# q and k of batches 2 to 7 made feature-major by TensorE transposes instead of a DMA crossbar round trip

## Chip, core and metric

One core of one Trainium2 chip runs the kernel in a single launch. The metric is the device time of that core in microseconds. The times of a kernel are given as the median of its runs; the profile is one execution, recorded by the hardware profiler.

Engines: PE is TensorE's matmuls, PEld its weight loads, DVE is VectorE, ACT ScalarE, POOL GpSimd, SP SyncE, which here only issues transfers. Each engine takes its instructions in order. PSUM is the memory that TensorE writes; SBUF is the on-chip memory for the rest.

## What is computed

Blockwise causal attention over 8 batches of 8 heads, 576 positions and 64 features, followed by a gated linear unit whose gate is a causal convolution of five taps:

```
scores = scale * np.matmul(q, k.transpose(0, 1, 3, 2))     # scale = 1/8
mask = block_i >= block_j                                  # blocks of 64 positions
attn = softmax of scores where mask
x = np.matmul(attn, v)                                     # (8, 8, 576, 64)
x = x.transpose(0, 2, 1, 3).reshape(8, 576, 512)
gate_pre[:, s] = sum over k of conv_w[k] * x[:, s + k - 4]
gate = 1 / (1 + exp(-gate_pre))
out = (gate * (x @ w_val)) @ w_out                         # float32, (8, 576, 512)
```

## The kernel before

Two heads are worked on at a time, 64 features each, so that a pair fills the 128 partitions. A step t is one pair of heads: batch b = t // 4, pair n = t % 4; there are 32 steps with scores, and nine more (LAG = 9), as the gated unit runs nine steps behind. The gated unit's step m = t - 9 makes one group of 128 features of one batch.

**What a step holds**, in the order in which it is written and in which TensorE takes it:

- `scores(t, 0)`: score matmuls k x q into the PSUM tile `ps` (pool psS, two buffers), and the exponentials on ACT into `pt` (L205)
- on every second step, `load_pair` loads q and k of a half-batch `hb` (two pairs of heads) on SP, and GpSimd casts them to half precision into `q16` (L118); `load_v` and `cast_v` do the same for v once a batch
- `project`: four matmuls into `ot`, a copy by ACT into `ob` (L393), and a transfer of `ob` to the output, issued from ACT's own queue (L394)
- on the first step of a batch, `den`: 88 small matmuls into `dn`, the sums of the softmax of the batch before, and their reciprocal `ri` on DVE; `spread` copies it to `rqs` on GpSimd a step later
- on the last step of a batch and on the first of the next, `pv` for two pairs: a shuffle of the reciprocals into `rb` on DVE, matmuls into `x`, and a product of `x` and `rb` into `xb` on DVE
- `scores(t, 1)` and `scores(t, 2)`: the other score matmuls and exponentials (L231, L205)
- from t = 9 on, `gate`: ten matmuls into `cv` and a tanh on ACT; then `val`: eight matmuls into `vp` and a product on DVE into `gv`

The tiles `tr`, `dn`, `x`, `cv`, `vp` and `ot` share one PSUM pool, psG, of four buffers; a tile gets a buffer when the reader of an earlier one is done with it.

**Order.** Every matmul and transpose on TensorE goes through `tc.keep_in_program_order`. So does every DVE operation that is written as `vec.…` (class `Ordered`; its operations carry line 56), and every load on SP (`load`, line 46). Engines wait for each other by semaphores that the framework puts in.

**Feature-major q and k.** The scores need q and k with features on partitions: `qkT`, a tile of two buffers, one per batch. There are two ways to it. Half-batches 0 to 3 (batches 0 and 1) take `trans(hb, part)`: six TensorE transposes of 128 x 128 into the PSUM tile `tr` (L169), and one or two copies from there into `qkT`, on DVE but for one on ACT. Three parts make a half-batch. Half-batches 4 to 15 (batches 2 to 7) take the other way: `store_rows(hb)` writes the cast q and k to a tensor `qk_scratch` in device memory by two transfers on SP, on even steps, and `cross(hb)` issues two crossbar transposes on SP on the following odd step (L157), which read the scratch and write `qkT`. Half-batch hb serves the steps 2 hb and 2 hb + 1; it is stored in step 2 hb - 4 and crossed in step 2 hb - 3. The number XB = 2 sets where one way ends and the other begins.

The list `tr` of a step holds its parts: on an even step parts 1 and 2 of half-batch t/2 + 1, on an odd step part 0 of half-batch (t + 3)/2. Until t = 8 they are put between the parts of the scores; from t = 9 on, where a step has any, one would follow `gate`, and the next `val`.

Of the kernel before, what the change touches and what calls it, by code (L numbers as in the profile page):

```python
# [10 lines left out]
def kernel(  # L11
# [20 lines left out]
    nc = tc.nc  # L32
    fp32 = mybir.dt.float32
    fp16 = mybir.dt.float16
# [4 lines left out]
    B, H, S, D = q.shape  # L39
    NT = B * 4  # L40

    def mm(**kw):
        tc.keep_in_program_order(nc.tensor.matmul(**kw))  # L43

    def load(**kw):
        tc.keep_in_program_order(nc.sync.dma_start(**kw))  # L46
# [36 lines left out]
    qkp = ctx.enter_context(tc.tile_pool(name="qkp", bufs=2))  # L83
# [21 lines left out]
    q16 = {}  # L105
# [15 lines left out]
    def load_v(b):  # L121
        st = vstp.tile([128, 36, 64], fp32, tag="vst")
        load(out=st[:, :, :], in_=v[b].rearrange("h s d -> (h s) d").rearrange(
            "(t p) d -> p t d", p=128))
        vsts[b] = st
# [14 lines left out]


    qkT = {}
    scr = nc.dram_tensor("qk_scratch", [B, 2, 4, S, 128], fp16, kind="Internal")

    def store_rows(hb):
        b, half = divmod(hb, 2)
        for w in range(2):
            load(out=scr[b, w, 2 * half:2 * half + 2].rearrange("n (x c) d -> x n (c d)", c=9),
                 in_=q16[hb, w][:, :, :, :].rearrange("p c z d -> p (c z d)"))

    def cross(hb):

        b, half = divmod(hb, 2)
        if b not in qkT:
            qkT[b] = qkp.tile([128, 2, 4, S], fp16, tag="qkT", name="qkT")
        for w in range(2):
            tc.keep_in_program_order(nc.sync.dma_start_transpose(  # L157
                out=qkT[b][:, w, 2 * half:2 * half + 2, :].rearrange("p n s -> p (n s)"),
                in_=scr[b, w, 2 * half:2 * half + 2].rearrange("n s d -> (n s) d")))

    def trans(hb, part):

        b, half = divmod(hb, 2)
        if b not in qkT:
            qkT[b] = qkp.tile([128, 2, 4, S], fp16, tag="qkT", name="qkT")
        tr = psG.tile([128, 6, 128], fp16, tag="G")
        slots = [divmod(6 * part + s, 9) for s in range(6)]
        for s, (w, c) in enumerate(slots):
            tc.keep_in_program_order(nc.tensor.transpose(  # L169
                out=tr[:, s, :], in_=q16[hb, w][:, c, :, :], identity=ident16[:, :]))  # L170
        for w in range(2):
            ss = [s for s in range(6) if slots[s][0] == w]
            if ss:
                c0 = slots[ss[0]][1]
                evac = nc.scalar.copy if hb == 0 and part == 1 else vec.tensor_copy
                evac(
                    out=qkT[b][:, w, 2 * half:2 * half + 2, :].rearrange(
                        "p n (x c) -> p n x c", c=9)[:, :, :, c0:c0 + len(ss)],
                    in_=tr[:, ss[0]:ss[-1] + 1, :].rearrange("p c (x n) -> p n x c", n=2))

# [6 lines left out]
    def first_q(h, i):  # L187
        return 2 * i + 1 + h

    def scores(t, part):  # L190
        b, n = divmod(t, 4)
        if part == 0:
            pts[t] = ptp.tile([128, 2880], fp16, tag="pt", name="pt")
        pt = pts[t]
        hs = (slice(0, 64), slice(64, 128))
        qT = [qkT[b][hs[h], 0, n, :] for h in range(2)]
        kT = [qkT[b][hs[h], 1, n, :] for h in range(2)]

        def full(ps, h, i, lo):
            f = 64 * first_q(h, i)  # L200
            mm(out=ps[:, h, lo:lo + S - f], lhsT=kT[h][:, f - 64:f + 64], rhs=qT[h][:, f:S],
               start=True, stop=True, skip_group_check=True)

        def ex(o, src, w):
            nc.scalar.activation(out=pt[:, o:o + w], in_=src, func=AF.Exp, bias=0.0,  # L205
                                 scale=0.125)

        if part == 0:
            ps = psS.tile([128, 2, 512], fp32, tag="S")
            full(ps, 0, 0, 0)  # L210
            full(ps, 1, 0, 0)
            full(ps, 1, 3, 448)
            ex(0, ps[:, :, :], 1024)
            ps = psS.tile([128, 2, 512], fp32, tag="S")
            full(ps, 0, 1, 0)
            full(ps, 1, 1, 0)
            full(ps, 0, 3, 384)
            full(ps, 1, 2, 320)
            ex(1024, ps[:, :, :], 1024)
            return  # L220
        q4 = [x.rearrange("d (j x) -> d j x", x=64) for x in qT]
        if part == 1:
            ps = psS.tile([128, 2, 512], fp32, tag="S")
            full(ps, 0, 2, 0)
            mm(out=ps[64:128, 1, 0:256], lhsT=kT[1][:, 0:64], rhs=q4[1][:, 1:8:2, :],
               start=True, stop=True, skip_group_check=True)
            for i in range(4):
                f = 64 * (2 * i + 1)
                mm(out=ps[0:64, 1, 64 * i:64 * i + 64], lhsT=kT[1][:, f:f + 64],
                   rhs=qT[1][:, f:f + 64], start=True, stop=True, skip_group_check=True)  # L230
            nc.scalar.activation(  # L231
                out=pt[:, 2048:2560].rearrange("p (h x) -> p h x", h=2),
                in_=ps[:, :, 0:256], func=AF.Exp, bias=0.0, scale=0.125)
            return
        ps = psS.tile([128, 2, 512], fp32, tag="S")
        mm(out=ps[64:128, 0, 0:320], lhsT=kT[1][:, 0:64], rhs=q4[1][:, 0:9:2, :],
           start=True, stop=True, skip_group_check=True)
        for i in range(5):
            f = 128 * i
            mm(out=ps[0:64, 0, 64 * i:64 * i + 64], lhsT=kT[0][:, f:f + 64],  # L240
               rhs=qT[0][:, f:f + 64], start=True, stop=True, skip_group_check=True)
        ex(XO, ps[:, 0, 0:320], 320)
# [178 lines left out]
    def load_pair(hb):  # L421
        if hb < 2 * B:
            for w in range(2):
                load_qk(hb, w)
# [3 lines left out]
    for part in range(3):  # L428
        trans(0, part)
# [2 lines left out]

    proj = []
    LAG = 9
    XB = 2
    for t in range(NT + LAG):
        b, r = divmod(t, 4)
        m = t - LAG
        hb = (t + 3) // 2 if t % 2 else t // 2 + 1
        tr = [(hb, part) for part in ((1, 2), (0,))[t % 2]] if hb < 2 * XB else []  # L440
        if t == 0:
            tr.insert(0, (1, 0))
        if t < NT:
            scores(t, 0)
        if t % 2 == 0:
            load_pair(t // 2 + 3)
        if t % 2 == 0 and 2 * XB <= t // 2 + 2 < 2 * B:
            store_rows(t // 2 + 2)
        if t % 2 == 1 and 2 * XB <= t // 2 + 2 < 2 * B:
            cross(t // 2 + 2)  # L450
        if r == 0 and b < B:
            load_v(b)
        if t in (2, 3, 6, 7):
            weights(t // 4, t % 2 * 2)
        if r == (2 if b else 1) and b < B:
            cast_v(b)
        if t <= 4:
            conv_weights(t - 1)
        if proj:
            project(*proj.pop(0))  # L460
        if r == 0 and 1 <= b <= B:
            den(b - 1)
        if m < 0 and tr:
            trans(*tr.pop(0))
        for n in range(2):
            if r == 3 and 1 <= b <= B:
                pv(4 * b - 4 + n)
            if r == 0 and 2 <= b <= B + 1:
                pv(4 * b - 6 + n)
            if n == 0 and t < NT:  # L470
                if 0 <= m:
                    scores(t, 1)
                    scores(t, 2)
                else:
                    scores(t, 1)
                    if tr:
                        trans(*tr.pop(0))
        if m < 0 and t < NT:
            scores(t, 2)
        if r == 1 and 1 <= b <= B:  # L480
            spread(b - 1)
        if 0 <= m < NT:
            gate(*divmod(m, 4))
        if tr:
            trans(*tr.pop(0))
        if 0 <= m < NT:
            val(*divmod(m, 4))
            u, i = divmod(m, 8)
            if i == 3:
                proj.extend((u, j) for j in range(4))  # L490
            if i == 7:
                proj.extend((u, j) for j in range(4, 9))
        if tr:
            trans(*tr.pop(0))
        if proj:
            project(*proj.pop(0))
# [32 lines left out]
```

## Time and profile before

| | |
|---|---|
| median of 3 runs | 280.26 us (279.19 to 280.95) |
| the profiled run | 280.95 us, its span 278.8 us |
| mean granted TensorE clock | 0.920 |
| PE busy | 217.4 us, 78% |
| PEld busy | 146.6 us, 53% |
| ACT busy | 139.3 us, 50% |
| DVE busy | 118.2 us, 42% |
| POOL busy | 116.6 us, 42% |
| transfers from SP's queue (q1) | 44.57 MB, 61.4% of 16 engines |
| transfers from ACT's queue (q10) | 9.45 MB, 9.1% |
| scratch stores | 24 of 288 KB, 5.6 us from issue to landing |
| crossbar transposes | 24, 4.4 us from issue to landing |

Busy time is time with an instruction in work; matmuls are pipelined, so their durations overlap, and the time that a run of them takes is read from the start of one to the start of the next. In the rows of a timeline the first number is the start in microseconds from the start of the span, the second the duration; `[9.24 <-ACT pt L205]` says that the engine was idle for 9.24 us before this row, until ACT's instruction on `pt` released it. In the rows of groups, `x8 | 7.6, 950` is eight instructions, 7.6 us in all, 950 ns each.

The page's 40 slices (7 us each) show how the clock and the transfers run along the span:

```profile
PEclk9999975599989799995699777999999999999999
DMA  6998589999868995999899989988730210031214
```

The transfer engines are nearly full for the first two thirds, as long as q and k are loaded, and the granted clock dips in that part several times.

### The profile page before, as it was taken

How to read it: one execution, taken by the hardware profiler on the slowest of the kernel's cores; microseconds unless marked ns; L12 is line 12 of the kernel's file. 1: busy time of each engine (PE TensorE's matmuls, PEld its weight loads, DVE VectorE, ACT ScalarE, POOL GpSimd, SP SyncE). 2: the span in 40 equal slices, each digit the busy share in tenths (PEclk: the TensorE clock that was granted, in tenths of full speed). 3: DMA queues.
4: the chain of work that ended last, by engine and by line, in shares of the span. 5: the costliest groups of instructions: out<-in, count | busy, mean ns of one | idle time of the engine just before them, and what ended most of it. 6: DMA issues, size and time to landing. Idle time of an engine off the chain costs nothing.

```text
span 278.8 us, 6862 instructions
## 1 busy us (share of the span) xinstructions
PE 217.4 (78%) x2848; PEld 146.6 (53%) x2848; DVE 118.2 (42%) x249; ACT 139.3 (50%) x233; POOL 116.6 (42%) x168
## 2 busy tenths in 40 slices
PE   0599873968486889880798485989998998899994
PEld 0465642846273457540476243665467457567671
DVE  2278972445152145610248010672257136648230
ACT  2558681377143585450563534546664682342433
POOL 5455953864474357073807363139005800400000
PEclk9999975599989799995699777999999999999999
DMA  6998589999868995999899989988730210031214
GB/s 188 347 269 245 171 283 195 312 245 299 179 212 157 355 282 214 243 296 137 319 246 281 186 282 274 278 181 160 156 128 2 78 75 5 24 126 41 100 54 188
DMA packets 56745, 54.46 MB, mean 195 GB/s; under 512 B 30597, under 2 KB 39813, under 8 KB 56714
## 3 DMA queue, kind: packets, MB, share of 16 engines
q1 hardware_dynamic: 51520, 44.57, 61.4%
q10 hardware_dynamic: 5194, 9.45, 9.1%
q8 instruction: 22, 0.36, 0.5%
q14 instruction: 9, 0.07, 0.1%
HBM read 30.42 MB, written 16.52 MB: 168 GB/s over the span
## 4 chain that ended last, share of the span: by engine, by line
PE 55%; ACT 14%; DMA 13%; DVE 7%; SPq 6%; issue 3%; ACTq 0%; DVEq 0%
PE cv L43 15%; ACT pt L205 12%; PE vp L43 11%; PE ps L43 10%; PE ot L43 7%; DMA qkT<-qk_scratch 5%; PE x L43 5%; DMA qk_scratch<-t 5%; PE dn L43 5%; SPq L157 4%; DVE ri L56 3%; SPq L46 2%; PE tr L169 2%; DMA st<-in_k_dram 2%; DVE rb L56 2%
## 5 line engine op out<-in xcount | busy, mean ns | idle before, releaser
L205 ACT ACTIVATE pt<-ps 128x1024 f16<-128x1024 f32 (+1 forms) x96 | 76.4, 828 | 46.1 <-PE ps L43 24.1
L43 PE MATMUL ps<-qkT 64*64 64x64 f16 (+10 forms) x608 | 52.5, 268 | 41.6 <-ACT pt L205 30.0
L56 DVE SCALAR_TENSOR_TENSOR gv<-th,vp 128x288 f16<-128x288 f32 x64 | 28.9, 454 | 109.2 <-PE vp L43 95.7
L43 PEld LDWEIGHTS <-qkT 64*64 64x64 f16 (+1 forms) x608 | 26.0, 108 | 70.5 <-issue 54.9
L118 POOL CAST t<-st 128x1152 f16<-128x1152 f32 x30 | 34.3, 1146 | 45.7 <-DMA st<-in_q_dram 34.7
L365 ACT ACTIVATE th<-cv 128x288 f32<-128x288 f32 x64 | 26.2, 411 | 38.8 <-PE cv L43 37.6
L43 PEld LDWEIGHTS <-diag 128*128 128x128 f16 x320 | 31.2, 102 | 15.3 <-issue 4.4
L43 PE MATMUL ot<-w_out_sb,gv 128*128 128x512 f16 x144 | 35.8, 380 | 0.7 <-ACT th L365 0.7
L393 ACT COPY ob<-ot 128x512 f32<-128x512 f32 x36 | 21.2, 588 | 29.7 <-PE ot L43 28.7
L43 PE MATMUL x<-pt,t 128*64 128x256 f16 (+3 forms) x384 | 28.5, 261 | 2.2 <-DVE ri L56 2.2
L43 PEld LDWEIGHTS <-w_val_sb 128*128 128x128 f16 x256 | 26.0, 101 | 8.1
L131 POOL CAST t<-st 128x2304 f16<-128x2304 f32 x8 | 16.9, 2106 | 31.4 <-DMA st<-in_v_dram 31.2
L231 ACT ACTIVATE pt<-ps 128x512 f16<-128x512 f32 x32 | 19.5, 610 | 14.5 <-PE ps L43 14.4
L56 DVE RECIPROCAL ri<-dn 128x288 f32<-128x288 f32 x8 | 15.7, 1956 | 22.7 <-PE dn L43 22.7
L296 POOL COPY rq_71<-ri 32x288 f32<-32x288 f32 x32 | 13.5, 423 | 25.5 <-DVE ri L56 24.3
L43 PEld LDWEIGHTS <-t 128*64 128x64 f16 x384 | 19.3, 115 | 6.6 <-issue 4.9
L43 PEld LDWEIGHTS <-gv 128*128 128x128 f16 x144 | 13.4, 98 | 14.5 <-issue 3.1
L43 PE MATMUL cv<-xb_67,diag 128*128 128x288 f16 x120 | 19.1, 312 | 1.8 <-DVE xb_68 L56 1.8
L296 POOL COPY rq_70<-ri 32x288 f32<-32x288 f32 x28 | 11.8, 423 | 17.9 <-DVE ri L56 16.8
L43 PE MATMUL cv<-xb_68,diag 128*128 128x288 f16 x120 | 17.6, 295 | 1.3 <-DVE xb_69 L56 1.3
L43 PEld LDWEIGHTS <-oh 128*32 128x32 f16 x704 | 14.8, 110 | 2.3 <-issue 2.3
L43 PE MATMUL dn<-pt,oh 128*32 128x160 f16 (+7 forms) x704 | 15.8, 254 | 0.0
(55 smaller groups left out, 246.3 us busy)
## 6 DMA issues: line engine op xcount, KB each, us to landing
st<-in_q_dram SPq DMA_DIRECT2D x32, 288.0 KB, 4.2
st<-in_k_dram SPq DMA_DIRECT2D x32, 288.0 KB, 5.2
out_dram<-ob ACTq DMA_DIRECT2D x36, 256.0 KB, 2.5
qk_scratch<-t SPq DMA_DIRECT2D x24, 288.0 KB, 5.6
st<-in_moe_w_val_dram SPq DMA_DIRECT2D x2, 512.0 KB, 7.3
st<-in_moe_w_out_dram SPq DMA_DIRECT2D x2, 512.0 KB, 5.5
qkT<-qk_scratch SPq DMA_TRANSPOSE x24, 4.4
st<-in_v_dram SPq DMA_DIRECT2D x8, 0.2 KB, 10.1
```

Of the source, the lines that this page charges most:

```text
L43: tc.keep_in_program_order(nc.tensor.matmul(**kw))
L46: tc.keep_in_program_order(nc.sync.dma_start(**kw))
L56: return lambda **kw: tc.keep_in_program_order(f(**kw))
L118: cast(out=t[:, :, :, :], in_=st[:, :, :, :].rearrange("p z c d -> p c z d"))
L131: nc.gpsimd.tensor_copy(out=t[:, :, :], in_=st[:, :, :])
L157: tc.keep_in_program_order(nc.sync.dma_start_transpose(out=qkT[b][:, w, 2 * half:2 * half + 2, :].rearrange("p n s -> p (n s)"), in_=scr[b ...
L169: tc.keep_in_program_order(nc.tensor.transpose(out=tr[:, s, :], in_=q16[hb, w][:, c, :, :], identity=ident16[:, :]))
L205: nc.scalar.activation(out=pt[:, o:o + w], in_=src, func=AF.Exp, bias=0.0, scale=0.125)
L231: nc.scalar.activation(out=pt[:, 2048:2560].rearrange("p (h x) -> p h x", h=2), in_=ps[:, :, 0:256], func=AF.Exp, bias=0.0, scale=0.125)
L296: move.tensor_copy(out=rqs[b % 2][r0:r0 + 32, e, :], in_=ri[r1:r1 + 32, :])
L365: nc.scalar.activation(out=th[:, HF * hf:HF * hf + HF], in_=cv[:, :], func=AF.Tanh, bias=0.0, scale=0.5)
L393: nc.scalar.copy(out=ob[:, :], in_=ot[:, :])
```

## The change

The crossbar way is taken out: `qk_scratch`, `store_rows` and `cross` go, and with them 24 stores and 24 crossbar transposes on SP. `trans` serves all 16 half-batches (the bound of XB becomes B): 36 more parts of six TensorE transposes, and 48 more copies out of PSUM on DVE, at the places in the steps that are told above. The two middle axes of `qkT` change places, from (q or k, pair) to (pair, q or k). The class `Ordered` and the `vec` that keep VectorE to its written order are the same in both kernels.

```diff
     qkT = {}
-    scr = nc.dram_tensor("qk_scratch", [B, 2, 4, S, 128], fp16, kind="Internal")
-
-    def store_rows(hb):
-        b, half = divmod(hb, 2)
-        for w in range(2):
-            load(out=scr[b, w, 2 * half:2 * half + 2].rearrange("n (x c) d -> x n (c d)", c=9),
-                 in_=q16[hb, w][:, :, :, :].rearrange("p c z d -> p (c z d)"))
-
-    def cross(hb):
+
+    def trans(hb, part):
 
         b, half = divmod(hb, 2)
         if b not in qkT:
-            qkT[b] = qkp.tile([128, 2, 4, S], fp16, tag="qkT", name="qkT")
-        for w in range(2):
-            tc.keep_in_program_order(nc.sync.dma_start_transpose(
-                out=qkT[b][:, w, 2 * half:2 * half + 2, :].rearrange("p n s -> p (n s)"),
-                in_=scr[b, w, 2 * half:2 * half + 2].rearrange("n s d -> (n s) d")))
-
-    def trans(hb, part):
-
-        b, half = divmod(hb, 2)
-        if b not in qkT:
-            qkT[b] = qkp.tile([128, 2, 4, S], fp16, tag="qkT", name="qkT")
+            qkT[b] = qkp.tile([128, 4, 2, S], fp16, tag="qkT", name="qkT")
         tr = psG.tile([128, 6, 128], fp16, tag="G")
...
-                    out=qkT[b][:, w, 2 * half:2 * half + 2, :].rearrange(
+                    out=qkT[b][:, 2 * half:2 * half + 2, w, :].rearrange(
...
-        qT = [qkT[b][hs[h], 0, n, :] for h in range(2)]
-        kT = [qkT[b][hs[h], 1, n, :] for h in range(2)]
+        qT = [qkT[b][hs[h], n, 0, :] for h in range(2)]
+        kT = [qkT[b][hs[h], n, 1, :] for h in range(2)]
...
     LAG = 9
-    XB = 2
...
-        tr = [(hb, part) for part in ((1, 2), (0,))[t % 2]] if hb < 2 * XB else []
+        tr = [(hb, part) for part in ((1, 2), (0,))[t % 2]] if hb < 2 * B else []
...
-        if t % 2 == 0 and 2 * XB <= t // 2 + 2 < 2 * B:
-            store_rows(t // 2 + 2)
-        if t % 2 == 1 and 2 * XB <= t // 2 + 2 < 2 * B:
-            cross(t // 2 + 2)
```

## The prediction

> **What bounds the kernel now.** I read the page's chain of waits first.
>
> ```profile
> PE 55%; ACT 14%; DMA 13%; DVE 7%; SPq 6%; issue 3%; ACTq 0%; DVEq 0%
> PE cv L43 15%; ACT pt L205 12%; PE vp L43 11%; PE ps L43 10%; PE ot L43 7%; DMA qkT<-qk_scratch 5%; PE x L43 5%; DMA qk_scratch<-t 5%; PE dn L43 5%; SPq L157 4%; DVE ri L56 3%; SPq L46 2%; PE tr L169 2%; DMA st<-in_k_dram 2%; DVE rb L56 2%
> ```
>
> TensorE is over half of the path, and 19% is transfers and the queue that issues them, mostly the round trip through `qk_scratch`. To see how it gets there, the same chain in order of time around its longest stop:
>
> ```profile
> 123.23 0.93 ACT pt L205
> ...
> 124.20 0.54 PE ps L43 x5
> 124.74 4.08 SPq L157
> ...
> 128.92 3.51 DMA qkT<-qk_scratch
> ...
> 132.50 0.34 ACTq L394
> ...
> 132.88 1.03 ACT pt L205
> ...
> 133.96 0.47 PE ps L43 x5
> ```
>
> The columns are start, duration (us) and what ran. The second exponential of t=18 (132.88) does not need the crossbar's data. It stands behind an output transfer on ScalarE's queue (L394), and that issue is held until the crossbar transposes in flight have landed. In TensorE's timeline the same stop reads so:
>
> ```profile
> 133.96 0.47 PE L43 MATMUL ps<-qkT 64*64 64x320 f16 x6 [9.24 <-ACT pt L205]
> 134.37 2.54 PE L43 MATMUL cv<-xb_69,diag 128*128 128x288 f16 x10
> ...
> 142.37 1.40 PE L43 MATMUL cv<-xb_69,diag 128*128 128x288 f16 x10
> ```
>
> 9.24 us idle, and the ten cv matmuls that follow take 2.54 us instead of 1.40: after a stop the array runs at half pace for a while. Then a stretch with such a stop beside one (t=25 to 28) without:
>
> ```profile
> 119.40:134.40 15.00, 5.67 (x47) 3.23 (x47) 0.91 (x2) 4.77 (x10) 8.83 (x15) 0.74 1.02 222
> ...
> 192.80:219.60 26.80, 24.24 (x349) 16.09 (x350) 11.88 (x25) 16.74 (x31) 9.53 (x17) 1.00 0.35 94
> ```
>
> Columns: length, busy us of PE, PEld, DVE, ACT, POOL, granted clock, DMA share, GB/s. Undisturbed, PE is busy 24.24 of 26.80 us at clock 1.00, with DVE at 11.88 and ACT at 16.74: TensorE is the bound, and the others have room.
>
> **The change part by part: what it removes.** By the starts of each batch's first score matmuls in TensorE's timeline and the chain (for the end of batch 7 the start of the last dn), batch 3 (t=12 to 15) lasts from 75.93 to 107.84, 31.9 us; batch 4 36.9 us (to 144.76); batch 5 36.4 (to 181.19); batch 6 26.84 (to 208.03); batch 7 25.79 (to 233.82). Batches 6 and 7 have no crossbar stop. A pair of batches has nine projections, of which odd batches run four and even ones five, so I set batches 3 and 5 against batch 7 and batch 4 against batch 6: lost 6.1, 10.1 and 10.6 us. Ahead of t=8 PE waits 4.75 us and ahead of t=12 4.1 us (71.83 to 75.93) for qkT. Sum 35.6 us. It agrees with the timeline's idle rows (4.75, 3.94, 3.51, 9.24, 3.72, 0.71, 3.30: 29.2) plus some 6 us of half-pace matmuls after them. All of it goes, as neither a scratch store, nor a transpose on SP, nor an output held by one is left. So without crossbar and before anything is added the span is 278.8 - 35.6 = 243.2 us. SP loses 24 stores and 24 transposes (up to 8.2 us of SP for one); the q and k loads queued behind them go out earlier, which only helps. Its queue's 44.57 MB shrink by 14.2 MB; the 30.4 MB left, at the 300 GB/s that slices of the page reach, need about 100 us of some 190, so loads stay hidden, as do POOL's casts (9.53 of 26.80).
>
> **What it adds on TensorE.** Twelve half-batches of three groups, 36 groups of six transposes. The trace has such groups already:
>
> ```profile
> 31.42 0.51 PE L169 MATMUL tr<-ident_59,t 128*128 128x128 f16 x6
> 31.86 0.52 PE L43 MATMUL ps<-qkT 64*128 64x256 f16 x6
> 32.31 0.51 PE L169 MATMUL tr<-ident_59,t 128*128 128x128 f16 x6
> 32.75 0.72 PE L43 MATMUL ps<-qkT 64*64 64x320 f16 x9
> ```
>
> Start to next start 0.44 us (31.42 to 31.86, 32.31 to 32.75); the chain has them at 0.75 to 0.79 before, when PE ran at half pace. Their mean of 294 ns is latency: six overlap in half a microsecond. Thirty groups belong to t=9 and later, where undisturbed PE runs at full pace: 30 x 0.45 = 13.5 us. They stand between cv and vp, and after vp, where PE has no wait to fill; the PE waits on ACT (0.41 us at each third part of the scores) come later in the step and start from the score matmuls themselves, so a group ahead of them only shifts them. I hide nothing there. Six groups fall in t=5 to 8, where ACT is the bound (8.09 busy of 9.2 us from 33.6) and PE idles some of each step: 6 x 0.75 = 4.5 at most, 0 at least; I take 3, since idle rows of 0.3 to 0.7 us cover less than a group.
>
> The Trainium skill, "TensorE: Matmul & The Clock Gate", Part 4, gives about 275 ns for one 128x128 transpose inside a kernel and says that transposes do not engage the full clock. Laid end to end that would be 216 x 0.275 = 59 us, a span of 303 and a slower kernel. The rows above show the duration but not the serial cost, so I don't use it.
>
> **What it adds on DVE and in PSUM.** Per half-batch two evictions of 768 columns and two of 384:
>
> ```profile
> L56 DVE COPY qkT<-tr 128x768 f16<-128x768 f16 x8 | 7.6, 950 | 4.0 <-PE tr L169 3.8
> ...
> L56 DVE COPY qkT<-tr 128x384 f16<-128x384 f16 x6 | 3.8, 702 | 1.3 <-PE tr L169 1.3
> ```
>
> 2 x 0.950 + 2 x 0.702 = 3.3 us, 6.6 a batch, on DVE's 11.9 of then some 30. The busy time is covered; what is queued behind an eviction matters. The tile of a group takes one of the four psG buffers that cv, vp, x, ot and dn share, until DVE has emptied it. On an even step the first group needs two evictions (1.40 us and a hand-over of 0.2), while vp and the second group give PE 0.98 + 0.45 us of other work: ot then waits about 0.2 us. vp's own products queue behind that eviction, and their buffers come free 1.4 us later; their next user stands an ot and the scores further on (0.86 + 0.54). On steps with two pv, shuffles (0.80 each) and the products into xb (0.49, 0.42) queue behind an eviction of 0.95, and PE arrives 0.45 later too; the buffers still come free ahead of cv by my count. The trace never shows groups beside cv and vp, so I bound this wait by 0 and by a whole eviction, 0.95 a group, and take 0.2 on ten even steps, 2 us, nearest to the count. The new order of qkT's two middle axes leaves rows and columns of each matmul contiguous as they are; cost nothing. VectorE keeps its written order in both kernels (`vec` is in both), so the words about shuffles name no edit.
>
> A crossbar transpose next to ordinary transfers needs nothing, says the skill ("DMA: Bandwidth & Descriptors", Rules for kernel authors), and "Advanced Engine Details and Errata", X-Bar Transpose, calls it as fast as a regular transfer. Read so, the removal would be worth little; the 9.24 us behind L394 show that in this program an ordinary output does wait for it.
>
> **Sum.** 243.2 + 13.5 + 3 + 2 = 261.7 span. The profiled run took 280.95 for its 278.8, so 2.15 lies around it: 263.9. It stands 0.69 above the median of 280.26: predicted 263.
>
> **The rivals.** (a) Some of the groups vanish in waits: the six early ones cost nothing, no buffer is waited for, and t=8, which ran its first half at half pace after a stop (dn 2.86 us against 1.61), gets about 1 us faster. 243.2 - 1 + 13.5 + 1.5 = 257; with a few more groups hidden, 255. For it: ACT's and DVE's waits in every step; against: the chain runs through PE. (b) PE stays at half pace for much of it: all 36 groups at 0.75 are 27 us: 243.2 + 27 + 2 + 1.5 = 274. For it: the clock of 0.73 from 33.6 to 42.8, without a long stop; against: clock 1.00 from 192.8 to the end. (c) Slower: the PSUM buffers decide. If each group makes PE wait for one eviction before cv, vp or ot gets a buffer, it costs 0.45 + 0.95 = 1.40, 50 us, and the time is 243.2 + 50 + 1.5 = 295. The break-even lies at 35.6 / 36 = 0.99 us a group. For it: four buffers for seven tiles a step, one strict DVE queue; against: DVE idles more than half of an undisturbed batch. (d) No change: the stops were a cover for something else that is as late, such as q and k loads behind a full DMA (share 0.91 to 1.02 in the disturbed stretches): 280. Against: share 0.35 once the round trip is over, though loads are then over too.
>
> **How the numbers follow.** Forecast (258 to 268) 0.60; (a) 0.13; (b) 0.16; (c) 0.08; (d) 0.03. Leaving out (c), (d) and the outer ends of (a) and (b), the range is 255 to 274. About 1% is what can be told from no change here. Faster 0.89, same 0.03, slower 0.08.
>
> **What would show it.** Right: no row of SP at L157, no wait of ACT on a transfer, clock 1.00 from about t=9 on, 288 transposes on PE in 48 groups at a pitch of 0.45 us, batches of 29 to 31 us all alike, PE busy about 230 us. Wrong: PE rows cv, vp or ot with idle ahead of them released by DVE qkT (rival c), a clock of 0.5 to 0.8 after t=9 (b), or POOL's casts waiting for loads with PE idle behind them (d).

## The result and the profile after

The changed kernel takes 263.75 us (median of 4 runs, 262.9 to 264.17) against 280.61 for the kernel before beside it: a ratio of 0.94, 95% interval 0.9353 to 0.9447. Here and below, a ratio compares fast runs with fast runs, while a median is of all runs. The prediction was 263. Its profiled run took 263.7 us, its span 261.9, where the prediction's sum was 261.7.

The chain of waits of the changed kernel, by engine and by line:

```profile
PE 54%; ACT 16%; DVE 15%; DMA 6%; issue 4%; SPq 1%; POOL 1%; ACTq 0%; DVEq 0%
PE cv L43 14%; ACT pt L188 13%; PE ps L43 9%; PE vp L43 9%; PE ot L43 8%; PE dn L43 5%; PE tr L152 5%; PE x L43 5%; DVE ri L56 4%; DMA st<-in_q_dram 4%; DVE rb L56 4%; DVE qkT L56 3%; DMA st<-in_k_dram 2%; ACT ob L376 2%; DVE xb_68 L56 1%
```

Transfers and SP's queue held 19% of the path and hold 7% now, and the lines with `qk_scratch` are gone. VectorE's share has doubled, and 8% are transposes and their evictions (the copies out of PSUM). But one line should not be there: 4% on a load of q. Two stretches of the same length of work, batch 4 and batch 6, in the windows of the changed kernel (columns as in the prediction):

```profile
98.04:132.80 34.76, 28.71 (x386) 19.59 (x388) 17.17 (x35) 16.91 (x29) 14.00 (x20) 0.90 0.60 187
...
160.90:190.25 29.35, 26.65 (x387) 18.16 (x388) 17.11 (x35) 16.75 (x29) 9.53 (x16) 1.00 0.32 87
```

Batch 6 is as forecast, at clock 1.00. Batch 4 is 5.4 us longer at clock 0.90. The chain in order of time has the reason:

```profile
114.48 0.71 SPq L46
...
115.29 9.96 DMA st<-in_q_dram
...
125.32 0.34 ACTq L377
...
125.71 1.03 ACT pt L188
...
126.78 0.48 PE ps L43 x5
```

It is the same picture as before, an output on ScalarE's queue (now L377), an exponential behind it, TensorE behind that, but what holds the output is a plain load of q. TensorE's row at 126.78 shows 3.62 us idle, and the ten cv matmuls after it take 2.58 us instead of the 1.41 before it. No crossbar is left in this kernel, so the prediction's reading of that wait ("held until the crossbar transposes in flight have landed") was too narrow. The kernel before had shown as much. Five of its exponentials stand behind a held output, and for one of them it is a load of k that holds it:

```profile
163.73 0.34 ACTq L394 DMA_DIRECT2D out_dram<-ob  x1
164.12 0.44 ACT L205 ACTIVATE pt<-ps 128x320 f16<-128x320 f32 x1 [3.88 <-DMA st<-in_k_dram]
```

The compiled programs say why. Transfers issued from SP and from ScalarE take their completion semaphores in turn from one set of eight, and a transfer that is to raise one first waits until the transfer that used it last has landed. Some of the changed kernel's transfers, numbered from 0 in the order of the program, with the semaphore that each waits for and the transfer that raised it last (an output also waits for its copy into `ob`):

```
49  SP   st<-in_q_dram  waits DMAHW1, raised last by 41 (a load of q)
50  SP   st<-in_q_dram  waits DMAHW2, raised last by 42 (a load of k)
56  ACT  out_dram<-ob   waits DMAHW0, raised last by 48 (a load of v)
58  ACT  out_dram<-ob   waits DMAHW2, raised last by 50 (a load of q)
82  ACT  out_dram<-ob   waits DMAHW2, raised last by 74 (a load of q)
```

Number 82 is the ninth output, the one issued at 125.32, and 74 is the load issued at 115.29 that lands at 125.25. The other stops fit too: in the profile of this kernel and in seven more (before, and of the runs below none, pe_only, cross_unread, before_xb8, after_again and after_merge) 19 exponentials wait behind a held output. Each time the transfer that the profile names, crossbar or load, is of the kind that the program makes that output wait for; in the kernel before these are four crossbar transposes and the one load of k. (The profile infers its releasers from semaphore events, so the two are not independent, but the times are measured: the load lands at 125.25, the output is issued at 125.32.)

From here on **theory A** is the prediction's: the stops come from the crossbar and go with it. **Theory B**: an output of ScalarE is held by any earlier transfer that shares its semaphore, loads included, and the crossbar only made such transfers more and later. The program's waits speak for theory B; the runs say what it is worth.

### The profile page after: what moved, and what is told of

Its sections match the earlier page's. It is cut to its first block, busy times and chain, and to the rows that moved or that the text cites. A ratio compares the mean times of both kernels' runs of the same rounds, so it can differ in the third digit from the quotient of the medians.

```text
span 261.9 us, 7260 instructions
## 1 busy us (share of the span) xinstructions
PE 222.4 (85%) x3064; PEld 153.8 (59%) x3064; DVE 149.2 (57%) x297; ACT 138.3 (53%) x233; POOL 116.0 (44%) x168
## 4 chain that ended last, share of the span: by engine, by line
PE 54%; ACT 16%; DVE 15%; DMA 6%; issue 4%; SPq 1%; POOL 1%; ACTq 0%; DVEq 0%
PE cv L43 14%; ACT pt L188 13%; PE ps L43 9%; PE vp L43 9%; PE ot L43 8%; PE dn L43 5%; PE tr L152 5%; PE x L43 5%; DVE ri L56 4%; DMA st<-in_q_dram 4%; DVE rb L56 4%; DVE qkT L56 3%; DMA st<-in_k_dram 2%; ACT ob L376 2%; DVE xb_68 L56 1%
## 5 line engine op out<-in xcount | busy, mean ns | idle before, releaser
L56 DVE COPY qkT<-tr 128x768 f16<-128x768 f16 (+1 forms) x62 | 49.3, 837 | 52.4 <-PE tr L152 52.3
L43 PE MATMUL ps<-qkT 64*64 64x64 f16 (+10 forms) x608 | 49.8, 256 | 17.7 <-ACT pt L188 14.5
L43 PEld LDWEIGHTS <-qkT 64*64 64x64 f16 (+1 forms) x608 | 24.9, 105 | 45.2 <-issue 38.0
L348 ACT ACTIVATE th<-cv 128x288 f32<-128x288 f32 x64 | 26.2, 410 | 39.1 <-PE cv L43 37.2
L56 DVE SCALAR_TENSOR_TENSOR gv<-th,vp 128x288 f16<-128x288 f32 x64 | 27.0, 447 | 26.5 <-PE vp L43 25.9
L43 PEld LDWEIGHTS <-diag 128*128 128x128 f16 x320 | 30.4, 100 | 14.2 <-issue 4.1
L152 PE MATMUL tr<-ident_59,t 128*128 128x128 f16 x288 | 27.3, 240 | 7.7 <-DVE ident_59 L94 6.5
L152 PEld LDWEIGHTS <-t 128*128 128x128 f16 x288 | 21.4, 108 | 12.0 <-DVE t L56 6.3
L43 PEld LDWEIGHTS <-w_val_sb 128*128 128x128 f16 x256 | 24.3, 98 | 5.5
L43 PEld LDWEIGHTS <-gv 128*128 128x128 f16 x144 | 12.7, 98 | 14.7 <-issue 2.1
L43 PE MATMUL cv<-xb_67,diag 128*128 128x288 f16 x120 | 18.0, 299 | 1.7 <-DVE xb_68 L56 1.7
```

Of the source, the lines that this page charges most:

```text
L56: return lambda **kw: tc.keep_in_program_order(f(**kw))
L152: tc.keep_in_program_order(nc.tensor.transpose(out=tr[:, s, :], in_=q16[hb, w][:, c, :, :], identity=ident16[:, :]))
L348: nc.scalar.activation(out=th[:, HF * hf:HF * hf + HF], in_=cv[:, :], func=AF.Tanh, bias=0.0, scale=0.5)
```

## The experiments

To compare profiles I use the start of the dn matmuls, once a batch. The length from one to the next is the length of a batch of steps:

| kernel | start of dn at t=12 | batch 3 | batch 4 | batch 5 | batch 6 | batch 7 | rest | span |
|---|---|---|---|---|---|---|---|---|
| before | 76.90 | 31.42 | 36.91 | 36.44 | 26.83 | 25.25 | 45.05 | 278.8 |
| changed | 70.43 | 28.08 | 34.77 | 28.10 | 29.34 | 26.21 | 44.97 | 261.9 |
| none | 67.55 | 29.22 | 36.20 | 25.81 | 26.82 | 25.26 | 45.04 | 255.9 |
| pe_only | 67.86 | 29.66 | 33.14 | 27.86 | 28.86 | 25.99 | 45.03 | 258.4 |
| cross_unread | 67.31 | 31.74 | 33.23 | 36.50 | 31.70 | 25.26 | 45.06 | 270.8 |
| before_xb8 | 72.39 | 28.09 | 34.49 | 28.08 | 29.34 | 26.22 | 44.99 | 263.6 |
| none_out_pool | 67.50 | 25.81 | 31.42 | 29.10 | 26.86 | 25.25 | 47.26 | 253.2 |
| after_out_pool | 73.44 | 28.09 | 29.40 | 28.09 | 29.40 | 26.20 | 47.18 | 261.8 |
| after_mix | 71.44 | 30.76 | 29.54 | 28.08 | 29.39 | 26.20 | 45.19 | 260.6 |

**Neither way.** From the changed kernel:

```diff
-        qT = [qkT[b][hs[h], n, 0, :] for h in range(2)]
-        kT = [qkT[b][hs[h], n, 1, :] for h in range(2)]
+        qT = [qkT[b % 2][hs[h], n, 0, :] for h in range(2)]
+        kT = [qkT[b % 2][hs[h], n, 1, :] for h in range(2)]
-        tr = [...] if hb < 2 * B else []
+        tr = [...] if hb < 4 else []
```

> Neither way is left for batches 2 to 7: no crossbar round trip, no transposes and no evictions; their scores read q and k of batches 0 and 1, so the output is not the reference's. Loads and casts stay. Theory A (the sum of the prediction: all 35.6 us lost to the crossbar go, nothing else holds): span 243, time 245. Theory B (ScalarE's outputs are held by any earlier transfer, loads too, because the transfers of both queues share eight completion semaphores): 245 plus one or more stops of 3 to 6 us behind loads, 248 to 256. Rival (the stops covered something as late): 270 or more.

Measured: 256.81 us (ratio to before 0.9164, 0.9089 to 0.9238). Theory A's 245 is missed by 12 us; theory B's 248 to 256 by 0.8. ScalarE's rows of this kernel still wait on loads, and TensorE's behind them:

```profile
85.03 1.02 ACT L188 ACTIVATE pt<-ps 128x1024 f16<-128x1024 f32 x1 [1.64 <-DMA st<-in_q_dram]
126.17 1.02 ACT L188 ACTIVATE pt<-ps 128x1024 f16<-128x1024 f32 x1 [6.67 <-DMA st<-in_q_dram]
```

```profile
86.11 0.34 PE L43 MATMUL ps<-qkT 64*64 64x320 f16 x6 [2.16 <-ACT pt L188]
...
127.24 0.47 PE L43 MATMUL ps<-qkT 64*64 64x320 f16 x6 [7.18 <-ACT pt L188]
```

Batches 5 and 6 are free of stops, 25.81 and 26.82; batches 3 and 4 exceed that by 3.4 and 9.4. Taken off, the span is 255.9 - 12.8 = 243.1. So the prediction's undisturbed 243.2 was right as a sum of undisturbed stretches, which no kernel ran at, and wrong as what is left when the crossbar goes: 12.8 us come to light, 9.34 of them idle behind the two held outputs, 1.80 in a stop of TensorE without a releaser in the profile (at 100.45), the rest mostly slower matmuls behind the stops.

**Transposes without evictions.** As none, but with the 36 groups, and for half-batches from 4 on no copy out of `tr`:

```diff
-        for w in range(2):
+        for w in range(2 if hb < 4 else 0):
             ss = [s for s in range(6) if slots[s][0] == w]
```

> As none, with the 36 groups of transposes of batches 2 to 7 on TensorE, whose products nobody reads: no evictions on VectorE, scores of batches 2 to 7 still from batches 0 and 1. Against none: +16.5 us by the prediction's 0.45 a group at full pace and 3 for the early ones; +10 to 12 by the pitch of about 0.33 that the rows of the changed kernel show (cv to vp 1.57 us with a group between, 1.24 without). What is left up to the changed kernel's 263.8 is the price of the evictions: 2 by the prediction; more than 5 would mean that PSUM buffers decide.

Measured: 260.22 us (0.9301, 0.9242 to 0.936), only 3.4 above none; both figures expected are missed, and the stops shrink at the same time (batch 4 is 3.1 us shorter than in none although TensorE has more to do). The undisturbed batches give the price: 27.86 - 25.81 and 28.86 - 26.82, 2.05 us for six groups, 0.34 each. The changed kernel's rows show it directly, against two rows of the same place of the kernel before, where no group stands between cv and vp:

```profile
67.24 1.40 PE L43 MATMUL cv<-xb_67,diag 128*128 128x288 f16 x10
68.48 0.49 PE L152 MATMUL tr<-ident_59,t 128*128 128x128 f16 x6
68.81 1.14 PE L43 MATMUL vp<-xb_67,w_val_sb 128*128 128x288 f16 x8
```

```profile
63.69 1.40 PE L43 MATMUL cv<-xb_67,diag 128*128 128x288 f16 x10
64.93 1.14 PE L43 MATMUL vp<-xb_67,w_val_sb 128*128 128x288 f16 x8
```

From cv to vp 1.57 us with the group and 1.24 without, 0.33. The start-to-start 0.44 that the prediction used had some of a gap in it that the following score matmuls have anyway: ahead of score matmuls a group of the changed kernel reads 0.43 (63.21 to 63.64), yet from vp to those matmuls it is 1.41 us with the group (from 62.23) and 1.08 without (56.81 to 57.89), again 0.33.

**The crossbar unread.** The kernel before, with the stores and transposes in place, but into a tile of their own, and the scores from batches 0 and 1 as above:

```diff
     def cross(hb):
-            qkT[b] = qkp.tile([128, 2, 4, S], fp16, tag="qkT", name="qkT")
+            qkT[b] = qkp.tile([128, 2, 4, S], fp16, tag="qkX", name="qkX", bufs=1)
```

> The kernel before with its stores and crossbar transposes all in place, but into a tile of their own that nobody reads; scores of batches 2 to 7 read q and k of batches 0 and 1 (output not the reference's). If the loss is the wait for late qkT alone (8.85 us and the slow matmuls after it would then be too little, so the idle rows must have been misread): near none. Theory A and B, most of the loss is ScalarE held behind transfers: only the waits at t=8 and t=12 go, 4.75 + 4.1 and about 3 of slow matmuls, 266 to 273.

Measured: 272.87 us (0.9745, 0.9673 to 0.9816), inside the range of both theories and far from none. Of the 24.2 us between before (280.97 beside it) and none, 8.1 go when no score waits for late data, and 16.1 come with the round trip's presence. The split is rough, as a transpose into a tile that nobody reads doesn't wait for TensorE either. ScalarE's rows name what it was held by, crossbar and loads in turn:

```profile
86.52 1.02 ACT L205 ACTIVATE pt<-ps 128x1024 f16<-128x1024 f32 x1 [2.97 <-DMA qkX<-qk_scratch]
...
117.04 0.44 ACT L205 ACTIVATE pt<-ps 128x320 f16<-128x320 f32 x1 [5.23 <-DMA st<-in_q_dram]
...
157.09 1.02 ACT L205 ACTIVATE pt<-ps 128x1024 f16<-128x1024 f32 x1 [4.66 <-DMA qkX<-qk_scratch]
```

**The axes of qkT.** The kernel before with `XB = B`:

> The kernel before with XB = 8: every half-batch through TensorE, the old order of qkT's axes. The same time as the changed kernel, 263.8 within 1, if the axes cost nothing; a difference above 2 would make the layout part of the result.

Measured: 265.69 us (0.9491, 0.9433 to 0.955), 1.9 above the expected. Its batches 3 to 7 are those of the changed kernel within 0.3; the difference stands before t=12 (72.39 against 70.43). The granted clock is lower there (0.76 against 0.92 from 54 to 69 us); what lowers it isn't shown. The changed kernel itself, run again on another chip:

> The changed kernel itself, unchanged, on the chip of these runs: 263.8 within 1. It is the measure for the other two of this set.

It gave 265.01 us (0.9508, 0.9377 to 0.964; runs from 262.95 to 266.64), 1.2 above the expected, with 69.68 to t=12 and 34.50 for batch 4. Its interval and that of the kernel with XB = B overlap; no price of the axes is shown.

**Outputs off ScalarE's queue.** One edit in three kernels (none, changed, before):

```diff
-        nc.scalar.dma_start(out=out2d[...], in_=ob[:, :])
+        nc.gpsimd.dma_start(out=out2d[...], in_=ob[:, :])
```

> As none (no crossbar, no transposes of batches 2 to 7, scores from batches 0 and 1), with the 36 output transfers issued from GpSimd's queue, whose transfers have completion semaphores of their own, in place of ScalarE's. Theory B: no row of ScalarE waits on a load any more, the stops of 2.2 and 7.2 us and the half-pace matmuls behind them go, and the time is the undisturbed sum: 245 to 248. Theory A's remaining rival (the 257 of none is made up of something other than ScalarE's held outputs): 254 to 260. If issuing from GpSimd delays its casts, stops of another kind appear and it is above 260.

Measured: 252.95 us (0.9044, 0.897 to 0.9118): below none, though the two intervals overlap a little, and above the 248, between the two theories. No exponential of ScalarE waits on a transfer, and batch 3 is at the undisturbed 25.81. But batches 4 and 5 have a stop of another kind, TensorE's vp waiting for ScalarE's copy of `ot` (2.88 and 2.44 us idle), which waits for an output on GpSimd's queue to free its buffer:

```profile
114.55 0.59 ACT L376 COPY ob<-ot 128x512 f32<-128x512 f32 x1 [4.47 <-DMA out_dram<-ob]
```

The rest is 2.2 us longer, behind the last output. Without these, 253.2 - 4.6 - 3.3 - 2.2 = 243.1 again.

> The changed kernel with its 36 output transfers issued from GpSimd's queue. Theory B: its one stop (3.6 us idle at 123 and slow matmuls behind it, together about 5.6) goes: 257 to 259. Theory A: no change, 263.8. Against none_out_pool it gives the price of 36 groups with evictions where nothing is stopped: 18.5 by the prediction (245.0 to 263.5), 12 to 14 by the pitch of 0.33.

Measured: 262.43 us (0.936, 0.9278 to 0.9442), not told apart from the changed kernel as a time; theory B's 257 to 259 is missed. The profile tells more: batch 4 takes 29.40 like batch 6, so its stop of 5.4 us is gone, as theory B has it; 2.2 us are given back at the end, and t=12 is reached 3.0 us later, for which I have no shown cause (the granted clock from 54 to 69 us is 0.73, against 0.92 in the changed kernel). Batches 3 to 7 are all undisturbed here. Against none's undisturbed 25.81, 26.82 and 25.26 they cost 10.7 us more for 26 groups, 0.41 a group with its evictions; against pe_only the evictions cost 0.23 in an odd batch and 0.54 in an even one.

> The kernel before, crossbar and all, with its 36 output transfers issued from GpSimd's queue. Theory B: the stops of 3.5, 9.2, 3.7 and 3.3 us behind ScalarE's held outputs go with their slow matmuls, the waits for qkT stay (4.75, 4.1 and slow matmuls): 256 to 265. Rival (the crossbar is late whoever issues the outputs, so the stops move to the score matmuls): 270 to 281.

Measured: 276.97 us (0.9858, 0.9759 to 0.9956). Theory B's 256 to 265 is missed, the rival's range holds it. The waits for qkT grew (6.59 and 4.28 us), and the held outputs took another way to TensorE. The chain of this kernel:

```profile
147.30 9.05 DMA st<-in_v_dram
...
158.56 4.28 DMA out_dram<-ob
...
162.94 0.59 ACT ob L393
...
163.57 1.12 PE vp L43 x4
```

GpSimd waits for a load of v before it can cast, the output stands behind the cast on its queue, ScalarE's copy waits for a buffer of `ob`, and vp for the PSUM buffer of `ot`. So with the transfers this full (DMA share 0.87 to 1.02 from 28 to 190 us) the late ones found another engine in line behind them.

**Three tries at the stop of the changed kernel.** Two buffers for the loaded v (`vstp`, `bufs=2`):

> The changed kernel with two buffers in place of one for the loaded v, so that a load of v need not wait until GpSimd has cast the v before it (SP waits 38.4 and 31.9 us for that cast in the changed kernel's trace, and the q and k loads stand behind it). Theory B: the loads go out earlier, ScalarE's output at 121 finds its semaphore free, the stop goes: 257 to 260. If the stop has another cause: 263.8. It also tries for a kernel faster than both.

Measured: 267.21 us (0.9535, 0.943 to 0.964). A miss: ScalarE's exponentials no longer wait on loads, but batches 4 and 5 are 34.76 and 30.84 us. The longest stop of TensorE is one for which the profile has no releaser:

```profile
105.86 0.48 PE L43 MATMUL x<-pt,t 128*64 128x256 f16 x4 [4.05 <-issue]
```

One load in place of two for q and for k of a half-batch:

```diff
-        for z in range(2):
-            load(out=st[:, z, :, :].rearrange("p c d -> p (c d)"),
-                              in_=src[z, :, 2 * half:2 * half + 2])
+        load(out=st[:, :, :, :].rearrange("p z c d -> p z (c d)"),
+             in_=src[:, :, 2 * half:2 * half + 2].rearrange("z x n f -> x n z f"))
```

> The changed kernel with each of q and k loaded by one transfer a half-batch in place of two (64 transfers of 288 KB become 32 of 576 KB; same bytes). The eight shared completion semaphores come round half as often. Theory B: ScalarE's outputs find their semaphore free, the stop of 5.4 us in batch 4 goes, nothing else changes: 257 to 260. If the stop follows the bytes in flight and not the number of transfers that share the semaphores: 263.8. It is also a try for a kernel faster than both.

Measured: 263.5 us (0.9333, 0.9165 to 0.9501; runs from 260.25 to 266.3), against 265.01 for the changed kernel beside it: not told apart. In the profile of the 261.04 us run the stop is smaller, not gone (batch 4 32.57 us), and the output is now held by a load of v:

```profile
123.96 1.02 ACT L187 ACTIVATE pt<-ps 128x1024 f16<-128x1024 f32 x1 [1.21 <-DMA st<-in_v_dram]
```

Outputs on SP in line with the loads (`load(out=out2d...)`), six buffers for `ob`:

> The changed kernel with the 36 output transfers issued from SP, in line with the loads, and six buffers in place of three for the copied output. ScalarE issues no transfer and can't be held by one. Theory B: the stop in batch 4 goes, 256 to 260, unless SP, which waits for GpSimd's casts, keeps six outputs back and ScalarE's copies then wait for a buffer: 262 to 270, with waits of ScalarE's copy on an output transfer in the rows.

Measured: 266.39 us (0.9545, 0.9428 to 0.9662), the slow branch of the expectation, though less by buffers than expected: one copy of ScalarE waits 2.34 us, until a load of k lands. TensorE has two long stops without a releaser (2.06 and 3.40 us) and one of 3.31 us put down to VectorE's shuffle.

**Both remedies.** The merged loads, and outputs from GpSimd for the first six batches, from ScalarE for the last two:

```diff
-        nc.scalar.dma_start(out=out2d[...], in_=ob[:, :])
+        (nc.gpsimd if u < 3 else nc.scalar).dma_start(out=out2d[...], in_=ob[:, :])
```

> The changed kernel with two edits: one load a half-batch for each of q and k (as in after_merge), and the outputs of the first six batches issued from GpSimd, those of the last two from ScalarE (the all-GpSimd version ended 2.2 us later behind the last output). Theory B: no row of ScalarE waits on a load, batch 4 takes 29.4 us like batch 6, the tail 45 us: span 243.1 + 13.5 = 257, time 257 to 260, the fastest of the set. If GpSimd's queue keeps outputs back, TensorE waits for ScalarE's copy of ot instead, 260 to 264.

Measured: 260.34 us in six runs (257.6 to 262.34), ratio 0.9266, 0.922 to 0.9312; the changed kernel's own interval begins at 0.9353. It is the fastest of the kernels that give the reference's output, 0.3 us above the 257 to 260 of theory B. Its profiled run is the longest of the six, 262.34 us; there batch 4 takes 29.54 us, and no exponential of ScalarE waits on a load, as expected; batch 3 has a stop of 2.24 us without a releaser.

## Why the prediction was right

The time was right to 0.3%, and the way to it half right: two terms were wrong and cancelled, so that closeness is luck. That it lies in the range is not: without the stop, or with the additions as dear as forecast, the time would be about 258 or 269, still within 255 to 274.

- **The undisturbed base**, 243.2: none and none_out_pool both give 243.1 after their stops are taken off (the two share the lengths of the undisturbed batches, so this is one finding rather than two).
- **"All of it goes, as neither a scratch store, nor a transpose on SP, nor an output held by one is left"** is the step that failed. It took what the chain named, the crossbar, for the only thing that can hold an output. Any transfer that raised the output's semaphore before it does, loads too. In none 12.8 us of stops were left, 9.34 of them idle time behind held outputs; in the changed kernel 5.4. Of the 29.2 us of idle rows that the prediction added up, one (0.71 at 164.91) already followed ScalarE's 3.88 us wait for a load of k. "No wait of ACT on a transfer", "clock 1.00 from about t=9 on" and "batches of 29 to 31 us all alike" were its tests, and all came out wrong: 3.1 us of ScalarE's idle time at 125.71, clock 0.92 from 54 to 70 us (t=9 to 11) and 0.90 in batch 4, batches of 26.2 to 34.8 us.
- **TensorE's price**: mis-sized. 0.45 a group was predicted for t=9 and later, 0.34 measured.
- **Early groups**: 3 us for six, and 1.8 for the four of t=9 to 11, with 0.2 for buffers: 5.0 up to t=12. The changed kernel reaches dn at t=12 2.9 us later than none; pe_only 0.3 later. That points to VectorE rather than TensorE: from 28 to 42 us VectorE is busy 10.71 of 14.00 us in none, 11.18 in pe_only and 13.35 in the changed kernel, with evictions between the reciprocal and the shuffle, and in the changed kernel's second profile (after_again) TensorE waits for one at t=8:

```profile
48.33 0.35 PE L43 MATMUL x<-pt,t 128*64 128x256 f16 x4 [0.65 <-DVE qkT L56]
```

  But the spread over kernels with the same work there (69.68 to 73.44) is as large as the term, so its size isn't shown.
- **Evictions**: 0.2 us on each even step, 0.4 a batch, against 0.23 and 0.54 measured. Their durations carried over, as the changed kernel's groups show:

```profile
L56 DVE COPY qkT<-tr 128x768 f16<-128x768 f16 x32 | 30.4, 954 | 29.1 <-PE tr L152 29.1
...
L56 DVE COPY qkT<-tr 128x384 f16<-128x384 f16 x30 | 19.3, 712 | 23.3 <-PE tr L152 23.3
```

- **The sum** by the measured terms: 243.1 + 2.9 + 10.7 + 5.4 = 262.1, against a span of 261.9. The additions were forecast at 18.5 and cost 13.6; the stop brought 5.4.
- **The rivals**: the PSUM buffers (c) didn't decide, the evictions' price is 0.23 to 0.54 us a batch and not 0.95 a group. Half pace (b) didn't last: from t=12 on the changed kernel's granted clock is below 1.00 only in batch 4, behind its stop. From 54 to 70 us it is 0.92, with no stop above 0.96 us there, and why isn't shown. (d), loads as late as the crossbar, was given 0.03 as a case of no gain; in part it is what happened. Without transposes the stops come to 12.8 us, with them to 5.4, so the 36 groups with evictions cost 263.75 - 256.81 = 7 us of time, half their 13.6. That part of TensorE's added work fills time in which it would have waited is my reading; no run takes it apart.
- **The skill's two rules.** "TensorE: Matmul & The Clock Gate", Part 4, would have put a transpose at about 275 ns and off the full clock; the runs show 0.34 us for six, and batches with six groups at clock 1.00. "DMA: Bandwidth & Descriptors", Rules for kernel authors, says that a transpose beside ordinary transfers needs nothing. The row is about transposes that corrupt each other's output, and says nothing of time; the prediction read it as a statement on time and took the 9.24 us stop as speaking against it. It does not: plain loads hold the outputs as well, by the program's semaphores.

Open: the stops of TensorE that have no releaser in the profile (1.97 us at 45.49 in the changed kernel, 4.05 in after_v2, 3.40 in after_out_sp6). No run took them apart, but the traces show what stands ahead of them. Queue q8, of kind "instruction", brings packets of 16 KB whose number goes with TensorE's instructions (22 where the page counts 2848 matmuls and as many weight loads, 24 where it counts 3064), so I take them for TensorE's program. After the first 8 us there are 16 such stops of 0.3 us or more in the profiles of all kernels, and each ends 1.3 to 1.6 us after one of these packets has landed. Ahead of after_v2's stop, which ends at 105.86, the transfers of the window 103 to 105 us hold this one:

```profile
q8 instruction: 1, 0.02, 3.7%
```

That TensorE waits there for its program is likely, then, and not shown: nothing was changed to test it. Also not tried: a set of completion semaphores for ScalarE's queue alone, the direct test of theory B; issuing from GpSimd, whose transfers raise semaphores of their own in the compiled program, stood in for it and changed more than that.

## What to carry to other kernels

When a wait of a compute engine is put down to a transfer, ask whether the engine needs that transfer's data. If it doesn't, look for a transfer that the engine itself issues, and in the compiled program for what that issue has to wait for. Here removing the transfer that was named handed the place to the next one in line. To say what a change is worth, run the kernel with neither the old nor the new way: its stops and its undisturbed batches separate what is removed from what is added, which the two totals alone can't do.

## What the runs showed of the hardware

Moving all outputs to GpSimd's queue made the end of the program 2.2 us longer (47.2 us against 45.0 from the last dn, in each of three pairs of kernels). Six fp16 transposes of 128 x 128 took 0.34 us of TensorE's time between matmuls at full clock, though each shows a mean duration of 240 ns. Every stop of TensorE of 0.3 us or more without a releaser ended 1.3 to 1.6 us after a 16 KB packet of the instruction queue had landed, 16 of 16.
